# Layer-norm transposes by DMA, quotients before the layer norm, and a higher target for zero matmuls, in a fused attention and feed-forward kernel on one core

## The chip, the cores and the metric

The kernel runs on one core of one Trainium2 chip. The metric is the device time of one execution in microseconds (us). The record marks every run told of here as undisturbed ("fast"), so that all may be compared, and all kernels gave correct results. Names of engines in the profile: PE is the tensor engine's matmuls, PEld its weight loads, DVE the vector engine, ACT the scalar engine, POOL GpSimd, SP the engine whose queue issues nearly all DMAs here. A "q" behind an engine (SPq) is its sequencer, issuing.

## The reference, cut to what matters

```python
B, S, D, H = 1, 2048, 640, 32            # head width 20; F = 1728; bf16 inputs
def reference(x, wqkv, wo, w_gate, w_up, w_down):
    h  = x + attention(layernorm(x), wqkv) @ wo     # 32 heads, softmax over 2048 keys, no mask
    n  = layernorm(h)
    return h + ((n @ w_gate) * (n @ w_up)) @ w_down
```

Both layer norms feed matmuls that contract over D. Their outputs lie with tokens on the partitions, and the matmuls need D on the partitions, so each tile of 128 tokens x 640 must be transposed.

## The kernel before

A Python program plans the whole schedule with model clocks (`pe_t`, `dve_t`, `act_t`) and writes out each engine's instructions in one fixed order. Each engine works through its list in order. The foreground is attention: PE makes a block of scores, ACT exponentiates two or three blocks at a time (E), PE multiplies E with the values (acc). Some blocks are exponentiated on DVE instead. The background (`bg`) is a generator of PE work that fills gaps: first all projections to keys, queries and values ("keys stage" below, while the flag `ingest` is set), then, for each of five chunks of queries (512, 512, 384, 384, 256), the output projection, the second layer norm and the feed-forward.

A transpose on PE, with its copy out of PSUM on DVE:

```python
def transposed(ln_t, dst):
    ln, t = ln_t
    t += LN_SLACK if attn and left else 0.0
    while t + T_SEM > pe_t + 0.05:
        yield ("until", t + T_SEM)
    yield from m_wait()
    pt, rec = m_take(BF16, [P, KC, P])
    for c in range(KC):                                   # 5 transposes of 128x128
        nc.tensor.transpose(pt[:, c, :], ln[:, c * P:(c + 1) * P], ident[:])
    pe(0.3)
    m_done(rec, copy_out(dst, pt, 0.35))
    yield 0.3
```

The keys stage, one pass for each 512 tokens (`after(n, g)` runs g, then n pieces of the next pass's layer norm):

```python
fill_kq()                       # 72 DMAs of constant rows, all at the start
for ch in range(NCH):
    ...
    yield from after(2, proj_pad(0, ch, 1)); yield from after(2, proj_pad(1, ch, 1))   # keys
    ...
    yield from after(3, proj_v(t0 + 2, 0))                                             # values
    if more: yield from trans(t0 + TPC)
    yield from after(9, proj_v(t0 + 3, 0))
    if more:
        for t in range(1, TPC): yield from trans(t0 + TPC + t)
```

The end of a chunk (in `second_stage`), and the rule for zero matmuls in the main loop. Zero matmuls add nothing to acc; they are meant to keep PE busy so that its clock stays up. A debt of at least one bank (512 columns) first calls background work forward, and only when there is none makes zeros:

```python
done.add(("Wo", ci)); hurry = False
if ci == len(CHUNKS) - 2:
    load_last()                 # 8 DMAs of 320 KB: weights for the last chunk
load_w(0); load_w(1)            # 4 DMAs of 160 KB
... ln_stats; ln_finish; ln_recip
for tt in range(ntt):
    lns.append(ln_apply(L, tt, hs[tt], xr[:, tt, :]))
    if tt > 0: yield from transposed(lns[tt - 1], ln2T[...])
yield from transposed(lns[-1], ln2T[...])
# main loop
debt = min(max(0.0, debt + (HAM0 if ci == 0 else HAM) * (T1 - T0) / 2 * 2370 - cols), 3 * BK)
while True:
    if not blocked and bg and (pe_t < T1 + over and credit > 0 or debt >= BK):
        ...bg_step()
    elif debt >= BK and acc_t is not None and (pe_t < T1 + over or not warm_pe):
        cmm(acc_t, zeros[:, 0:P], zeros[:], False, False, skip_group_check=True)
    else: break
```

The quotients (attention sums divided by their denominators) go a roundabout way: acc is copied to accS (DVE), the denominators are sent by DMA into rs, inverted on DVE (rr), sent through DRAM to rb, and POOL multiplies accS by rb into on. There are two accS buffers.

The softmax here doesn't subtract the row's maximum and nothing guards it: scores larger than these inputs give would overflow.

Of the kernel before, what the change touches and what calls it, by code (L numbers as in the profile page):

```python
# [17 lines left out]
P = 128  # L18
# [5 lines left out]
G = H // HP  # L24
NT = S // P
KC = D // P
BK = 512
NCH = S // BK
TPC = BK // P
# [3 lines left out]
NG0 = 2  # L33
# [12 lines left out]
LN_SLACK = 2.0  # L46
D_V = 0.72
T_ON = (6.5, 16.0)
HAM0 = 0.5
EPS_B = 1.0013580322265625e-05  # L50

T_SW = 0.095
T_SEM = 0.2
# [6 lines left out]
HAM = 0.50  # L60
# [13 lines left out]
def kernel(  # L74
# [11 lines left out]
    nc = tc.nc  # L86
# [21 lines left out]
    pe_t = 0.0  # L108
    dve_t = 0.0
    act_t = 0.0  # L110
    mode = "F"
    cols = 0.0
    attn = False
    hurry = False
    ingest = True
# [103 lines left out]
            for ch in range(NCH):  # L219
                nc.gpsimd.dma_start(r_[:, ch, :], t_[:])  # L220

    def fill_kq():
        k_src = rowk[:].rearrange("r c q -> r (c q)")
        q_src = rowq[:].rearrange("r c q -> r (c q)")
        for g in range(NG0, G):
            for j in range(HP):
                r0, r1 = 32 * j + DH, 32 * j + 32
                nc.sync.dma_start(kT[g][r0:r1, :], k_src)
                nc.sync.dma_start(qT0[r0:r1, g, :], q_src[:, 0:q0w])
                nc.sync.dma_start(qT1[r0:r1, g, :], q_src[:, q0w:S])  # L230
# [45 lines left out]
    def ln_apply(L, i, s, ln):  # L276
        nc.vector.tensor_scalar(ln, s, L["mv"][:, i, 0:1], L["rstd"][:, i:i + 1],
                                ALU.subtract, ALU.mult)
        return ln, dve(0.36)
# [61 lines left out]
# [7 lines that stand above are left out]
        for c in range(KC):  # L348
            nc.tensor.transpose(pt[:, c, :], ln[:, c * P:(c + 1) * P], ident[:])  # L349
        pe(0.3)  # L350
        m_done(rec, copy_out(dst, pt, 0.35))
        yield 0.3


    def mm_qk(ps, lhs, ch):
        sl = slice(ch * BK, (ch + 1) * BK)
# [70 lines left out]
    done = set()  # L427
# [3 lines left out]
    def lnT_dst(t):  # L431
        return lnT[:, :, t * P:(t + 1) * P]
# [8 lines left out]
    dve_t = 4.0  # L441
    act_t = 8.0
    L = ln_new(TPC)
# [13 lines left out]
    lns = [ln_apply(L, t, xt[0][:, t, :], xt[0][:, t, :]) for t in range(TPC)]  # L457
# [8 lines left out]

    def first_stage():
        nonlocal ingest
        fill_kq()

        lns = []
        ahead = deque()

        def ln_ahead(ch):
            L = ln_new(TPC)
            x = [xt[ch][:, t, :] for t in range(TPC)]
            lns.clear()
            for t in range(TPC):
                ahead.append(lambda t=t: ln_stats(L, t, x[t]))
            ahead.append(lambda: ln_finish(L))  # L480
            ahead.append(lambda: None)
            ahead.append(lambda: ln_recip(L))
            for t in range(TPC):
                ahead.append(lambda t=t: lns.append(ln_apply(L, t, x[t], x[t])))

        def after(n, gen):
            yield from gen
            for _ in range(min(n, len(ahead))):
                ahead.popleft()()

        def trans(t):
            while len(lns) <= t % TPC:
                ahead.popleft()()
            return transposed(lns[t % TPC], lnT_dst(t))

        first_dense = NG0 * HP * DH // P
        f0 = first_dense
        for ch in range(NCH):
            t0 = ch * TPC
            more = ch + 1 < NCH  # L500
            if more:
                ln_ahead(ch + 1)
            if ch == 0:
                yield from after(1, proj_pad(1, 0, 1))
                yield from after(0, proj_v(0, 0))
                yield from after(1, proj_pad(1, 0, 0))
                yield from after(2, proj_v(1, 0))
            else:
                yield from after(2, proj_pad(0, ch, 1))
                yield from after(2, proj_pad(1, ch, 1))  # L510
                if not more:
                    yield from proj_dense(f0, [0], 0)
                yield from after(2, proj_v(t0, 0))
                if not more:
                    yield from proj_dense(f0, [0, 1], 1)
                yield from after(2, proj_v(t0 + 1, 0))
            yield from after(3, proj_v(t0 + 2, 0))
            if more:
                yield from trans(t0 + TPC)
            yield from after(9, proj_v(t0 + 3, 0))  # L520
            if more:
                for t in range(1, TPC):
                    yield from trans(t0 + TPC + t)
        ingest = False
        yield from proj_dense(f0, [2, 3], 1)
        for ft in range(f0 + 1, KC):
            yield from proj_dense(ft, [0], 0)
            yield from proj_dense(ft, [0, 1], 1)
            if ft == KC - 2:
                for t in range(TPC):  # L530
                    yield from proj_v(t, 1)
            yield from proj_dense(ft, [2, 3], 1)
            if ft == KC - 2:
                load_wo()
                for t in range(TPC, NT):
                    yield from proj_v(t, 1)
        for g in range(NG0):
            for ch in range(1, NCH):
                yield from proj_pad(g, ch, 0)
        for ft in range(f0, KC):  # L540
            yield from proj_dense(ft, [1, 2], 0)
            yield from proj_dense(ft, [3], 0)
# [41 lines left out]
    def second_stage(ci, q0, qw, xr):  # L584
# [68 lines left out]
                ln_stats(L, tt - 1, hs[tt - 1])  # L653
        done.add(("Wo", ci))
        hurry = False
        if ci == len(CHUNKS) - 2:
            load_last()
        load_w(0)
# [7 lines left out]
        for tt in range(ntt):  # L666
            calm()
            lns.append(ln_apply(L, tt, hs[tt], xr[:, tt, :]))
            if tt > 0:
                yield from transposed(lns[tt - 1], ln2T[:, :, (tt - 1) * P:tt * P])  # L670
        yield from transposed(lns[-1], ln2T[:, :, qw - P:qw])
        if end:
            yield "rest"
        yield ("until", dve_t + T_SEM)
        for f in range(NF):
            M = min(P, FF - f * P)
            if f + 2 < NF:
# [196 lines left out]
    def emit_PV(s):  # L874
# [16 lines left out]
        if last:  # L891
# [11 lines left out]
                normalise(ci, q0, qw, g, sums.pop((ci, g)), t)  # L903
            acc_t = None

    sums = {}

    last_sum = []
# [105 lines left out]
    while n < len(units):  # L1014
        if n >= 6:
            values(units[n - 6][-1][0])
        n_slot = n
        cols = 0.0
        T0 = act_t
        emit_exp(n)  # L1020
        pe_t = max(pe_t, T0)
        T1 = act_t
        if n + 1 < len(units):
            T1 += len(units[n + 1]) * BANK_ACT + FIX_ACT
        if left:
            pe_t = max(pe_t, act_t + T_SEM)
            emit_S(len(units))
            if not ingest and ring[0]["t"] <= pe_t and dve_t < act_t + D_AHEAD and len(dq) < 2 and len(left) > 5 * HP:
                start_D()
        values()  # L1030
        for z in list(later):
            if z[0] <= max(dve_t, act_t) and all(t in done for t in z[2]):
                later.remove(z)
                z[1]()
        pump(act_t + 0.5)

        ci = steps[min(pv_next, len(steps) - 1)][0]
        if left:
            rest = sum(1 for b in left if steps[b[0]][0] == ci)
            rate = RUSH0 if hurry or ci == 0 else RUSH * max(bgw, 5.0) / max(rest / 2.8, 4)  # L1040
        credit = min(credit + rate, max(5 * rate, 2.0))
        for i in range(0, min(LOOK, len(left)), HP):
            if not all(t in done for t in tags_of(left[i][0])):
                credit = max(credit, 2.0)
        debt = min(max(0.0, debt + (HAM0 if ci == 0 else HAM) * (T1 - T0) / 2 * 2370 - cols), 3 * BK)
        blocked = False
        over = (OVER, OVER2)[n % 2]
        while True:
            tick()
            if not blocked and bg and (pe_t < T1 + over and credit > 0 or debt >= BK):  # L1050
                c0 = cols
                c = bg_step()
                if isinstance(c, tuple):
                    blocked = c[1] > max(T1 + over, pe_t + 0.1)
                    pe_t = pe_t if blocked else max(pe_t, c[1])
                else:
                    credit -= c
                    bgw -= c
                    debt = max(0.0, debt - cols + c0)
                pump(act_t + 0.5)  # L1060
            elif debt >= BK and acc_t is not None and (pe_t < T1 + over or not warm_pe):

                cmm(acc_t, zeros[:, 0:P], zeros[:], False, False, skip_group_check=True)
                pe(0.216, "C")
                debt -= BK
            else:
                break
        pump(act_t + 0.9)
        n += 1
# [48 lines left out]
```

## Time and profile before

1008.31 us, the median of 3 runs (1008.09 to 1011.38). The profiled run took 1005.8 us, of which the profile covers a span of 1004.1.

| | before |
|---|---|
| ACT busy | 861 us, of it 849 in 745 exponentials |
| ACT idle from the 1st to the 52nd exponential (keys stage, 22 to 123 us) | 43 us |
| mean PE clock 21 to 123 us | 0.80 |
| after the last exponential | 57 us |

The first two parts of the page of the kernel before: busy time of each engine, then the span in 40 slices with busy tenths, and PEclk, the clock granted to PE in tenths.

```profile
PE 867.8 (86%) x14133; PEld 368.4 (37%) x14134; DVE 751.3 (75%) x1290; ACT 861.3 (86%) x776; POOL 226.1 (23%) x263
...
ACT  3466599799989999999999999999979999989701
...
PEclk8778889999999999999989989999989999999989
```

ACT is at 9 tenths over most of the span. In the first five slices, the keys stage, it is not. The table by stretch gives that in numbers (columns: stretch, its length, busy us of PE, PEld, DVE, ACT, POOL with instruction counts, clock, DMA share, GB/s).

```profile
25.00:50.00 25.00, 19.07 (x219) 7.47 (x211) 13.48 (x35) 10.90 (x11) 1.05 (x1) 0.73 0.27 76
50.00:75.00 25.00, 19.42 (x215) 7.32 (x211) 11.61 (x30) 15.16 (x13) 1.00 (x1) 0.73 0.02 6
75.00:100.00 25.00, 19.46 (x239) 8.07 (x239) 11.91 (x31) 16.97 (x15) 1.01 (x1) 0.86 0.01 1
100.00:125.00 25.00, 17.74 (x231) 6.47 (x223) 7.63 (x13) 13.74 (x13) 1.11 (x1) 0.85 0.06 13
375.00:400.00 25.00, 22.72 (x285) 7.65 (x284) 22.22 (x35) 25.00 (x23) 6.18 (x7) 1.00 0.35 85
```

In the first four stretches ACT works 10.9 to 17.0 us of 25 at a clock of 0.73 to 0.86; later it works 25.0 of 25 at a clock of 1.0. The table of waits says what ACT waited for (us in total, times, longest), and shows a wait at chunk ends.

```profile
ACT E L807 <- PE acc L884: 40.7, 19, 4.4
...
PE acc L884 <- DVE accS L898: 5.9, 2, 3.2
...
DVE accS L898 <- POOL on_339 L947: 3.6, 2, 1.9
```

The timeline shows how the keys of the second 512 tokens come about (start, length, engine, line, operation, tiles, count, and in brackets the idle time before it and what ended it).

```profile
42.25 1.15 DVE L277 TENSOR_SCALAR xw<-xw,mv,rstd 128x640 bf16<-128x640 bf16 x3
...
42.94 1.25 PE L349 MATMUL mt<-ident,xw 128*128 128x128 bf16 x10
...
45.72 2.75 PE L148 MATMUL mt<-lnT,Wp 128*32 128x512 bf16 x24 [0.58 <-DVE lnT L328]
...
49.82 1.45 ACT L807 ACTIVATE E<-sp 128x1536 bf16<-128x1536 f32 x1 [4.36 <-PE acc L884]
```

The last step of the layer norm (L277), the transposes of its tiles on PE (L349), and the key projection (L148), which waited for the last copy out of PSUM (lnT, L328), stand in a row; ACT resumes at 49.82 after 4.36 us. And this is the end of the third chunk:

```profile
737.56 0.85 POOL L266 TENSOR_TENSOR den<-ve,half 128x3 bf16<-128x3 bf16 x1 [7.93 <-DVE ve L263]
738.37 0.99 POOL L947 TENSOR_TENSOR on_339<-accS,rb 128x384 bf16<-128x384 f32 x1
...
739.40 0.56 DVE L898 COPY accS<-acc 128x384 f32<-128x384 f32 x1 [1.93 <-POOL on_339 L947]
...
740.01 0.80 PE L884 MATMUL acc<-E,Vx 128*32 128x384 bf16 x9 [3.18 <-DVE accS L898]
...
743.20 1.02 ACT L807 ACTIVATE E<-sp 128x1024 bf16<-128x1024 f32 x1 [4.57 <-PE sp L784]
```

The copy to accS at 739.40 waits for a buffer, which the quotient on_339 frees, and POOL runs that only after the layer norm's den. PE waits 3.18 us for the copy, and ACT 4.57 us for the scores behind it.

### The profile page before, as it was taken

The page shows a single profiled execution, that of the slowest core. Times are in us where ns is not written, and L with a number is a line of the kernel's source. Part 1 is how long each engine was busy: PE and PEld are TensorE (multiplying, and loading weights), DVE is VectorE, ACT ScalarE, POOL GpSimd, SP SyncE. Part 2 cuts the span into 40 slices and gives each one's busy share as a digit, 9 for nine tenths or more (in the row PEclk, how much of TensorE's full clock was granted, in tenths as well). Part 3 has the DMA queues.
Part 4 walks back from the last instruction along what each step waited for, and adds up shares of the span by engine and source line. Part 5 has one row for each costly group of instructions (what it writes and reads, how often), then busy time and mean ns, then how long its engine had stood idle before and what let it go on. Part 6 is the DMA issues. An engine that isn't in the chain of part 4 may idle for free.

```text
span 1004.1 us, 32961 instructions
## 1 busy us (share of the span) xinstructions
PE 867.8 (86%) x14133; PEld 368.4 (37%) x14134; DVE 751.3 (75%) x1290; ACT 861.3 (86%) x776; POOL 226.1 (23%) x263
## 2 busy tenths in 40 slices
PE   7777798789977989998988899989978999879988
PEld 3223222322222323223434333334433444434566
DVE  4544367678869798988788888888888887888542
ACT  3466599799989999999999999999979999989701
POOL 4000021222213132222232222322222222232100
PEclk8778889999999999999989989999989999999989
DMA  6200011301111113330010122301123311343304
GB/s 224 75 5 1 13 42 39 75 14 33 35 40 47 40 39 84 79 88 13 33 46 11 36 56 58 73 14 44 46 43 69 64 31 52 82 103 79 86 28 82
DMA packets 121916, 53.26 MB, mean 53 GB/s; under 512 B 98026, under 2 KB 117066, under 8 KB 121770
## 3 DMA queue, kind: packets, MB, share of 16 engines
q1 hardware_dynamic: 120794, 49.75, 20.8%
q8 instruction: 110, 1.80, 0.8%
q10 hardware_dynamic: 720, 1.31, 0.3%
q14 instruction: 36, 0.29, 0.1%
q0 software_dynamic: 256, 0.10, 0.0%
HBM read 43.47 MB, written 2.98 MB: 46 GB/s over the span
## 4 chain that ended last, share of the span: by engine, by line
ACT 40%; issue 23%; PE 21%; DVE 7%; SPq 4%; DMA 3%; POOL 1%; DVEq 0%; POOLq 0%; ACTq 0%
ACT E L807 40%; PE mt L148 10%; PE sp L784 5%; SPq L406 3%; PE acc L884 3%; PE acc L148 1%; DVE v L840 1%; PE mt L349 1%; DVE v L842 1%; DVE fx L834 1%; DVE ed L845 1%; POOL uc L837 1%; DMA rs<-accS 1%; DMA rd<-rr 1%; DVE Vx L328 1%
## 5 line engine op out<-in xcount | busy, mean ns | idle before, releaser
L807 ACT ACTIVATE E<-sp 128x1536 bf16<-128x1536 f32 x745 | 849.2, 1352 | 81.0 <-PE acc L884 40.7
L837 POOL TENSOR_SCALAR uc<-fx 128x512 f32<-128x512 uint16 x185 | 160.9, 870 | 587.0 <-DVE fx L834 561.1
L884 PE MATMUL acc<-E,Vx 128*32 128x256 bf16 (+3 forms) x2787 | 165.5, 321 | 7.9 <-DVE accS L898 5.9
L840 DVE SCALAR_TENSOR_TENSOR v<-fx 128x512 f32<-128x512 uint16 x185 | 156.0, 846 | 1.2
L834 DVE TENSOR_SCALAR fx<-mt 128x512 int32<-128x512 f32 x185 | 126.4, 684 | 32.9 <-PE mt L784 31.3
L842 DVE SCALAR_TENSOR_TENSOR v<-v,uc 128x512 f32<-128x512 f32 x185 | 129.5, 701 | 14.9 <-POOL uc L837 12.1
L845 DVE SCALAR_TENSOR_TENSOR ed<-fx,v 128x512 uint16<-128x512 int32 x185 | 133.7, 724 | 1.3
L884 PEld LDWEIGHTS <-Vx 128*32 128x32 bf16 x3072 | 57.9, 97 | 79.8 <-issue 72.3
L148 PE MATMUL mt<-ln2T,wg 128*32 128x512 bf16 (+1 forms) x1080 | 76.3, 360 | 1.0 <-DMA wg<-in_B_w_gate_dram 0.9
L148 PE MATMUL mt<-ln2T,wu 128*32 128x512 bf16 (+1 forms) x1080 | 73.7, 356 | 0.9 <-DVE gs L328 0.7
L884 PE MATMUL acc<-ed,Vx 128*32 128x256 bf16 (+3 forms) x285 | 69.2, 315 | 0.3 <-DVE ed L845 0.3
L148 PE MATMUL acc<-zeros 128*32 128x512 bf16 x676 | 62.3, 426 | 0.0
L328 DVE COPY gs<-mt 128x512 f32<-128x512 f32 (+3 forms) x54 | 33.6, 623 | 15.4 <-PE mt L148 15.3
L784 PE MATMUL sp<-qT_161,kT_152 32*128 32x256 bf16 (+3 forms) x284 | 29.2, 305 | 10.7 <-ACT E L807 10.4
L148 PEld LDWEIGHTS <-wu 128*32 128x32 bf16 x1190 | 27.2, 95 | 29.1 <-issue 17.9
L784 PE MATMUL sp<-qT_161,kT_155 32*128 32x256 bf16 (+3 forms) x287 | 29.6, 313 | 9.2 <-ACT E L807 8.7
L148 PEld LDWEIGHTS <-wg 128*32 128x32 bf16 x1190 | 27.4, 96 | 27.7 <-issue 17.6
L784 PEld LDWEIGHTS <-kT_153 32*128 32x128 bf16 x384 | 16.9, 92 | 53.4 <-issue 52.9
L784 PE MATMUL sp<-qT_161,kT_154 32*128 32x256 bf16 (+3 forms) x294 | 28.7, 292 | 8.8 <-ACT E L807 8.1
L784 PE MATMUL sp<-qT_161,kT_156 32*128 32x256 bf16 (+3 forms) x294 | 29.0, 292 | 8.0 <-ACT E L807 7.4
L324 ACT COPY gs<-mt 128x256 f32<-128x256 f32 (+3 forms) x16 | 6.2, 385 | 34.4 <-PE mt L148 34.4
L784 PE MATMUL sp<-qT_161,kT_158 32*128 32x256 bf16 (+3 forms) x291 | 28.3, 293 | 7.7 <-ACT E L807 6.8
(210 smaller groups left out, 1245.9 us busy)
## 6 DMA issues: line engine op xcount, KB each, us to landing
wg<-in_B_w_gate_dram SPq DMA_DIRECT2D x57, 160.0 KB
wu<-in_B_w_up_dram SPq DMA_DIRECT2D x57, 160.0 KB
rb<-rd SPq DMA_DIRECT2D x16, 256.0 KB
rb<-rd SPq DMA_DIRECT2D x16, 192.0 KB
out_dram<-xr SPq DMA_DIRECT2D x14, 160.0 KB
Wd<-in_B_w_down_dram SPq DMA_DIRECT2D x13, 160.0 KB
xr<-in_A_x_dram SPq DMA_DIRECT2D x2, 640.0 KB
qT_161<-in_B_w_gate_dram SPq DMA_DIRECT2D x4, 320.0 KB
```

The source lines that it names most:

```text
L148: nc.tensor.matmul(out[j:j + 32], lhsT=lhsT[:, j:j + 32], rhs=rhs, start=start, stop=stop, **kw)
L328: nc.vector.tensor_copy(dst, src)
L349: nc.tensor.transpose(pt[:, c, :], ln[:, c * P:(c + 1) * P], ident[:])
L406: nc.sync.dma_start(dst, tmp[lo - ft * P:hi - ft * P, 0:n])
L784: nc.tensor.matmul(out[:, c:c + n], lhsT=kT[g][32 * j:32 * j + 32, kt * P:(kt + 1) * P], rhs=q_of(g, q0 + qo, n)[32 * j:32 * j + 32, :], s ...
L807: nc.scalar.activation(E[:, 0:len(u), :], sp[:, 0:len(u), :], ACT.Exp, scale=LN2_ / UNIT, bias=-BIAS * LN2_ / UNIT)
L834: nc.vector.tensor_scalar_mul(fx[:], d["sp"], 512.0)
L837: nc.gpsimd.tensor_scalar(d["uc"][:], u, EXP_C, 0.0, ALU.mult, ALU.add)
L840: nc.vector.scalar_tensor_tensor(d["v"][:], d["u"], EXP_A, d["u"], ALU.add, ALU.mult)
L842: nc.vector.scalar_tensor_tensor(d["v"][:], d["v"][:], EXP_B, d["uc"][:], ALU.add, ALU.mult)
L845: nc.vector.scalar_tensor_tensor(e[:], d["fx"][:], 1.0 / 512.0, d["v"][:], ALU.mult, ALU.add)
L884: nc.tensor.matmul(acc_t[32 * j:32 * j + 32, qo:qo + n], lhsT=Vx[:, kt, h * VS:h * VS + 32], rhs=E_of[s, j][0][:, c:c + n], start=kt == k0 ...
```

## The change

Its intent: transposes leave PE and DVE and become DMA transposes on the SP queue (all but the first tiles and the last chunk's); the layer norm of the keys stage runs earlier and the filling of constant rows is split, so that the transposes don't stand behind 72 DMAs; quotients that are due are issued before the chunk's layer norm; and the target for zeros is 0.8 of PE's columns, but only in the keys stage.

```diff
-HAM0 = 0.5
+HAM0 = 0.8
+T_TR = 4.5
...
+    def transposed_dma(ln_t, dst):
+        nc.sync.dma_start_transpose(out=dst, in_=ln_t[0])
+        return ln_t[1] + T_TR
...                                                       # first_stage
-        fill_kq()
             for t in range(TPC):
-                ahead.append(lambda t=t: lns.append(ln_apply(L, t, x[t], x[t])))
+                def last(t=t):
+                    t_ln[ch] = transposed_dma(ln_apply(L, t, x[t], x[t]), lnT_dst(ch * TPC + t))
+                ahead.append(last)
         for ch in range(NCH):
+            while ahead:
+                ahead.popleft()()
+            while t_ln.get(ch, 0.0) > pe_t:
+                yield ("until", t_ln[ch])
+            fill_kq(range(min(NG0 + 2 * ch, G), min(NG0 + 2 * ch + 2, G)))
...                                                       # counts for after() of ch 0: 1,0,1,2 -> 2,1,2,3
-            yield from after(3, proj_v(t0 + 2, 0))
-            if more:
-                yield from trans(t0 + TPC)
-            yield from after(9, proj_v(t0 + 3, 0))
-            if more:
-                for t in range(1, TPC):
-                    yield from trans(t0 + TPC + t)
+            yield from after(4, proj_v(t0 + 2, 0))
+            yield from after(11, proj_v(t0 + 3, 0))
...                                                       # second_stage
         hurry = False
+        run_later()                                       # quotients that are due
...
-            if tt > 0:
+            if not end:
+                t = transposed_dma(lns[tt], ln2T[:, :, tt * P:(tt + 1) * P])
+            elif tt > 0:
                 yield from transposed(lns[tt - 1], ln2T[:, :, (tt - 1) * P:tt * P])
...
+        while t > pe_t:
+            yield ("until", t)
...                                                       # main loop
-        debt = min(max(0.0, debt + (HAM0 if ci == 0 else HAM) * (T1 - T0) / 2 * 2370 - cols), 3 * BK)
+        debt = min(max(0.0, debt + (HAM0 if ingest else HAM) * (T1 - T0) / 2 * 2370 - cols), 3 * BK)
```

More of the change, by code (lines that the diff above doesn't have):

```diff
@@ L220, in const_rows, with fill_kq @@
                 nc.gpsimd.dma_start(r_[:, ch, :], t_[:])
-    def fill_kq():
+    def fill_kq(gs):
         k_src = rowk[:].rearrange("r c q -> r (c q)")
         q_src = rowq[:].rearrange("r c q -> r (c q)")
-        for g in range(NG0, G):
+        for g in gs:
             for j in range(HP):
@@ L468, in first_stage @@
         nonlocal ingest
-        fill_kq()
-        lns = []
+        t_ln = {}
         ahead = deque()
@@ L476, in ln_ahead @@
             x = [xt[ch][:, t, :] for t in range(TPC)]
-            lns.clear()
             for t in range(TPC):
@@ L489, in after @@
                 ahead.popleft()()
-        def trans(t):
-            while len(lns) <= t % TPC:
-                ahead.popleft()()
-            return transposed(lns[t % TPC], lnT_dst(t))
         first_dense = NG0 * HP * DH // P
@@ L503, in first_stage @@
             if ch == 0:
-                yield from after(1, proj_pad(1, 0, 1))
-                yield from after(0, proj_v(0, 0))
-                yield from after(1, proj_pad(1, 0, 0))
-                yield from after(2, proj_v(1, 0))
+                yield from after(2, proj_pad(1, 0, 1))
+                yield from after(1, proj_v(0, 0))
+                yield from after(2, proj_pad(1, 0, 0))
+                yield from after(3, proj_v(1, 0))
             else:
@@ L668, in second_stage @@
             lns.append(ln_apply(L, tt, hs[tt], xr[:, tt, :]))
-            if tt > 0:
+            if not end:
+                t = transposed_dma(lns[tt], ln2T[:, :, tt * P:(tt + 1) * P])
+            elif tt > 0:
                 yield from transposed(lns[tt - 1], ln2T[:, :, (tt - 1) * P:tt * P])
-        yield from transposed(lns[-1], ln2T[:, :, qw - P:qw])
         if end:
+            yield from transposed(lns[-1], ln2T[:, :, qw - P:qw])
             yield "rest"
-        yield ("until", dve_t + T_SEM)
+            t = dve_t + T_SEM
+        while t > pe_t:
+            yield ("until", t)
         for f in range(NF):
@@ L904, in emit_PV, with run_later @@
             acc_t = None
+    def run_later():
+        for z in list(later):
+            if z[0] <= max(dve_t, act_t) and all(t in done for t in z[2]):
+                later.remove(z)
+                z[1]()
     sums = {}
@@ L1030 @@
         values()
-        for z in list(later):
-            if z[0] <= max(dve_t, act_t) and all(t in done for t in z[2]):
-                later.remove(z)
-                z[1]()
+        run_later()
         pump(act_t + 0.5)
```

## The prediction

> **What bounds it now.** Mostly ScalarE's exponentials: the page gives ACT 861 of 1004 us busy, and the table of 25 us windows shows ACT at 25.0 of 25 in most windows from 325 to 725 us. Its idle time lies in three places. (a) While keys are made (22 to 125 us) ACT is busy only 11 to 17 of each 25 us, about 43 us idle; the granted clock is 0.73 to 0.86 there, 1.0 later. The waits are 39 us for value products (E <- acc) and 10 us for scores. The chain of waits in 22 to 130 us holds 51 us of projections, scores and value products, 5.7 us of PE transposes, 1.9 us of their copies. (b) At ends of chunks: 4.6 us at 743, 3.9 us at 885. The timeline shows the copy of the sums (accS) waiting for the quotient on_339, which POOL runs only after the layer norm's den. (c) The tail after 945 us, which stays.
>
> **What the change does.**
> - Keys stage: 12 tiles lose 5 transposes (0.6 us of PE per tile) and a 0.49 us DVE copy. Each becomes a DMA transpose on the SP queue, planned at 4.5 us after the layer norm, which is issued earlier. Keys then wait for one landing, not for transposes and copies in series (chunk 1: layer norm ends 43.4, key projection starts 45.7, ACT resumes 49.8). With the layer norm 4 to 5 us sooner and the flight partly hidden behind value projections, I expect 3 to 5 us per chunk, 11 us for three.
> - Zeros: the target 0.5 becomes 0.8 in this stage; it also calls background work earlier. A 512-column matmul is 0.38 us warm, 0.61 to 0.63 cold in this trace; the Trainium skill's "TensorE: Matmul & The Clock Gate" (Part 1: The HAM clock gate) says that the clock follows recent activity. I expect the clock to rise from 0.8 to about 0.92: 7 us off the 51 (51 x (1 - 0.8/0.92)), less some 4 us of added zeros: net 3 us.
> - Later chunks: 14 tiles lose 0.6 us of PE and 0.48 us of DVE. PE has slack there; DVE's 7 us let 2 or 3 more blocks be exponentiated on DVE (2.9 us each), worth 1 us.
> - Quotients first: at 739 and 882 the copy of the sums can start 1.7 us sooner, and the score behind two transposes about 1 us sooner: 4 us together.
>
> Sum: 19 us, shaded to 17 for late landings. ScalarE's work hardly changes; the gain is its idle time.
>
> **Risk.** No trace here has a DMA transpose. The skill's "VectorE: DVE Perf Modes" (The three transpose paths) gives 1309 ns for 128x128 by DMA; five in series would be an estimated 6.5 us, over the planned 4.5. PE works in order, so late landings would stop scores too, in 7 places.
>
> **Prediction:** 991 us, 8 in 10 between 977 and 1003. Faster by over 2%: 0.40; within 2%: 0.56; slower: 0.04.
>
> **What would show it.** Right: ACT idle in 22 to 125 us falls by 12 us or more; clock there over 0.9; the first score of group 2 (122 us) comes about 14 us sooner; the waits of accS for on_339 vanish; transposes land within 4.5 us. Wrong: PE waiting for lnT or ln2T from DMA over 2 us per chunk; zeros on the chain over 6 us; SP issue over 1 us per transpose, delaying the sums' DMAs, so that ACT idles more at chunk ends or between 125 and 325 us.

## The result

996.31 us, the median of 4 runs (994.53 to 997.16), against 1009.09 of the kernel before (4 runs). The ratio is 0.9868, with a 95% interval of 0.9844 to 0.9891. Ratios here are the mean time of one kernel's runs over that of the other's runs of the same rounds, so they are not quite the ratio of the medians. The page of the changed kernel, the same lines:

```profile
PE 862.5 (87%) x14051; PEld 358.0 (36%) x14052; DVE 749.7 (75%) x1273; ACT 861.0 (87%) x775; POOL 232.4 (23%) x265
...
ACT  4486779999898999999999899999979999869701
...
PEclk8798789999998899999989999999979998979999
```

And its stretches while keys are made, where the stage now ends at 109 us and not at 123:

```profile
25.00:50.00 25.00, 18.33 (x208) 6.19 (x204) 13.11 (x35) 11.91 (x11) 1.05 (x1) 0.72 0.34 65
50.00:75.00 25.00, 18.99 (x283) 7.46 (x279) 14.40 (x41) 22.04 (x20) 2.01 (x2) 0.97 0.34 76
75.00:100.00 25.00, 19.27 (x254) 6.36 (x246) 7.83 (x14) 16.72 (x15) 0.00 (x0) 0.90 0.14 30
```

ACT's busy time is the same to 0.3 us; what fell is its idle time. The second stretch shows it best: ACT 22.0 us where it was 15.2, at a clock of 0.97 where it was 0.73. Over the whole run its waits for acc fell from 40.7 to 24.4 us, while those for scores (sp) rose from 32.7 to 41.1 us, and PE has new ones, for a transposed tile (table of waits of the changed kernel):

```profile
ACT E L813 <- PE acc L890: 24.4, 13, 3.2
...
PE mt L149 <- DMA ln2T<-xr: 9.4, 2, 6.9
```

What the trace has of the tile lnT in the changed kernel lists its DMA transposes by the tile that they read (time to issue one, min/median/max in ns, then first and last start in us):

```profile
L357 SPq DMA_TRANSPOSE lnT<-xw x4: 1201/1227/1337, 32.8 to 40.9; - x4
...
L357 SPq DMA_TRANSPOSE lnT<-x_97 x4: 1200/1227/1742, 72.6 to 78.4; - x4
```

And the same of the tile ln2T, in the chunks:

```profile
L357 SPq DMA_TRANSPOSE ln2T<-xr x14: 1215/1246/1725, 337.3 to 877.7; - x14
```

The SP queue needs about 1.2 us to issue one. Three in a row start at 1.3 us distance; where PE waited for the last of them, it started 2.8 us after that one's issue began.

**Where the time went.** All kernels run 744 to 746 exponentials in nearly the same sequence, so the n-th exponential is a clock on which two traces can be laid side by side. How much sooner it started in the changed kernel's profiled run (us, worked out from the two traces):

| exponential | 1st | 31st | 51st (first of group 2) | 183rd | 201st | 251st | 661st | 701st | end |
|---|---|---|---|---|---|---|---|---|---|
| sooner by | 1.6 | 10.6 | 13.9 | 21.1 | 22.2 | 14.2 | 14.6 | 5.1 | 8.9 |

So in this trace the change gained 14 us in the keys stage, as predicted, and 7 to 8 us more in the stretch after it, which I had not predicted; then it gave back 8 us around the first chunk's end and 9.5 us around the fourth's, and won 4 us after the 701st exponential. The second loss is easy to see in the timeline of the changed kernel (start, length, engine, line, operation, tiles, count, idle time before it and what ended it):

```profile
869.23 1.84 DVE L278 TENSOR_SCALAR xr<-h,mv,rstd 128x640 bf16<-128x640 f32 x3
...
871.20 1.00 SPq L606 DMA_DIRECT2D wu<-in_B_w_up_dram  x1
...
872.30 2.64 SPq L943 DMA_DIRECT2D rs<-accS  x4
...
875.04 3.92 SPq L357 DMA_TRANSPOSE ln2T<-xr  x3
...
880.47 0.83 PE L149 MATMUL mt<-ln2T,wg 128*32 128x384 bf16 x8 [6.85 <-DMA ln2T<-xr]
...
881.95 1.45 ACT L813 ACTIVATE E<-sp 128x1536 bf16<-128x1536 f32 x1 [7.27 <-PE sp L790]
```

The layer norm of all three tiles is done at 871.07. The three transposes start to be issued at 875.04, because loads of weights and the sums' DMAs stand ahead of them in the SP queue. From 863 us on the loads take 1.0 to 1.6 us each to issue, the four DMAs of the sums 2.64 us together. From the end of the layer norm to the tile's use 9.4 us pass, where the plan had 4.5. PE has the feed-forward's first matmul next in its list and stops for 6.85 us, scores behind it stop too, and ACT idles 7.27 us.

Such a lead is not measured to the last us, since each kernel has one trace. How far two traces differ can be seen from kernels whose program is the same up to there. In the kernel before, chunks_only, quot_only and wo_late (told of below) the first exponential came at 18.6 to 21.6 us and the 51st 101.6 to 105.0 us later. In the changed kernel, chunks_pe, keys_zeros, late_load and spread_load it came at 18.7 to 22.0 us and the 51st 89.3 to 92.4 us later. So the shorter keys stage is clear of this noise, but a difference of some 3 us between two kernels is not. late_load and spread_load have the changed kernel's program up to 860 us (the order of DMAs included). Their leads were 20.0 and 17.4 us at the 201st exponential and 14.6 and 14.5 at the 251st: what is given back there is anything from 3 to 8 us.

### The profile page after: what moved, and what is told of

Its sections match the earlier page's. It is cut to its first block, busy times and chain, and to the rows that moved or that the text cites. A ratio compares the mean times of both kernels' runs of the same rounds, so it can differ in the third digit from the quotient of the medians.

```text
span 995.2 us, 32806 instructions
## 1 busy us (share of the span) xinstructions
PE 862.5 (87%) x14051; PEld 358.0 (36%) x14052; DVE 749.7 (75%) x1273; ACT 861.0 (87%) x775; POOL 232.4 (23%) x265
## 4 chain that ended last, share of the span: by engine, by line
ACT 41%; PE 25%; issue 20%; DVE 7%; DMA 4%; SPq 3%; POOL 1%; POOLq 0%; DVEq 0%; ACTq 0%
ACT E L813 41%; PE mt L149 12%; PE sp L790 7%; PE acc L890 4%; SPq L412 3%; PE acc L149 1%; DVE st L254 1%; DVE ed L851 1%; DVE v L848 1%; DVE fx L840 1%; DMA rs<-accS 1%; DVE v L846 1%; DMA qT_161<-tmp 1%; DMA ln2T<-xr 1%; SPq L943 1%
## 5 line engine op out<-in xcount | busy, mean ns | idle before, releaser
L813 ACT ACTIVATE E<-sp 128x1536 bf16<-128x1536 f32 (+1 forms) x745 | 849.2, 1361 | 75.4 <-PE sp L790 41.1
L890 PE MATMUL acc<-E,Vx 128*32 128x256 bf16 (+3 forms) x2784 | 168.0, 325 | 5.7 <-DVE accS L904 3.5
L848 DVE SCALAR_TENSOR_TENSOR v<-v,uc 128x512 f32<-128x512 f32 x187 | 136.9, 735 | 11.0 <-POOL uc L843 7.9
L149 PE MATMUL mt<-ln2T,wg 128*32 128x512 bf16 (+1 forms) x1080 | 78.5, 368 | 11.7 <-DMA ln2T<-xr 9.4
L149 PE MATMUL mt<-ln2T,wu 128*32 128x512 bf16 (+1 forms) x1080 | 76.1, 362 | 0.1
L890 PE MATMUL acc<-ed,Vx 128*32 128x512 bf16 (+3 forms) x288 | 69.8, 313 | 1.6 <-DVE ed L851 1.6
L149 PE MATMUL acc<-zeros 128*32 128x512 bf16 x724 | 66.5, 422 | 0.0
L790 PE MATMUL sp<-qT_161,kT_155 32*128 32x256 bf16 (+3 forms) x290 | 30.6, 321 | 7.3 <-ACT E L813 7.2
L325 ACT COPY gs<-mt 128x256 f32<-128x256 f32 (+2 forms) x15 | 5.7, 380 | 32.1 <-PE mt L149 32.1
```

What stands on the lines that cost most here:

```text
L149: nc.tensor.matmul(out[j:j + 32], lhsT=lhsT[:, j:j + 32], rhs=rhs, start=start, stop=stop, **kw)
L790: nc.tensor.matmul(out[:, c:c + n], lhsT=kT[g][32 * j:32 * j + 32, kt * P:(kt + 1) * P], rhs=q_of(g, q0 + qo, n)[32 * j:32 * j + 32, :], s ...
L813: nc.scalar.activation(E[:, 0:len(u), :], sp[:, 0:len(u), :], ACT.Exp, scale=LN2_ / UNIT, bias=-BIAS * LN2_ / UNIT)
L848: nc.vector.scalar_tensor_tensor(d["v"][:], d["v"][:], EXP_B, d["uc"][:], ALU.add, ALU.mult)
L890: nc.tensor.matmul(acc_t[32 * j:32 * j + 32, qo:qo + n], lhsT=Vx[:, kt, h * VS:h * VS + 32], rhs=E_of[s, j][0][:, c:c + n], start=kt == k0 ...
```

## The experiments

Twelve kernels ran. All outputs are right. In each call the kernel before ran again on the same chip; its medians in the calls were 1004.8 to 1006.8 us, with runs from 999 to 1012, so an interval of a ratio is about 0.5% wide to each side.

| kernel | made from | ratio | 95% | median us | keys stage, us | ACT idle 641st to 721st exp. |
|---|---|---|---|---|---|---|
| before | | 1 | | 1005 to 1009 | 101.6 | 4.0 |
| changed | | 0.9868 | 0.984 to 0.989 | 996.3 | 89.3 | 12.5 |
| keys_only | before | 0.9828 | 0.978 to 0.988 | 990.2 | 91.3 | 10.9 |
| zeros_only | before | 0.9823 | 0.978 to 0.987 | 989.3 | 91.9 | 6.2 |
| chunks_only | before | 1.0106 | 1.005 to 1.016 | 1018.4 | 102.2 | 15.0 |
| quot_only | before | 1.0023 | 0.997 to 1.008 | 1009.2 | 105.0 | 7.0 |
| order_pe | before | 0.9870 | 0.982 to 0.992 | 993.6 | 99.1 | 8.1 |
| zeros_skip | zeros_only | 0.9960 | 0.989 to 1.003 | 999.7 | 96.5 | 6.2 |
| wo_late | before | 0.9975 | 0.991 to 1.004 | 1002.5 | 103.1 | 3.9 |
| no_zeros | changed | 0.9838 | 0.979 to 0.989 | 990.4 | 91.9 | 8.8 |
| chunks_pe | changed | 0.9859 | 0.980 to 0.992 | 991.7 | 89.7 | 6.6 |
| late_load | changed | 0.9897 | 0.985 to 0.994 | 996.2 | 92.4 | 12.8 |
| spread_load | changed | 0.9918 | 0.987 to 0.997 | 996.0 | 90.4 | 8.6 |
| keys_zeros | changed | 0.9884 | 0.985 to 0.992 | 993.1 | 89.9 | 6.1 |

"Keys stage" is the time from the 1st to the 51st exponential in the profiled run; it and the last column are worked out from the traces.

### The four parts alone

**keys_only**: the kernel before with the keys stage of the changed one (DMA transposes, earlier layer norm, split filling). The diff is that part of the change; the zeros stay at 0.5.

```diff
+ first_stage() as in the changed kernel, with transposed_dma
- HAM0 = 0.8
+ HAM0 = 0.5      (no run_later() in second_stage, chunks' transposes on PE)
```

> The kernel before with DMA transposes (and the layer norm order that goes with them) in the keys stage only; zeros at 0.5, quotients late, chunks' transposes on PE. Theory A (the gain is the keys stage's lost PE transposes and copies; the DMA transposes of later chunks give part of it back): the 51st exponential comes 10 to 15 us sooner than in the kernel before, as in the changed one, and the time is at or below the changed kernel's, ratio 0.978 to 0.988. Rival B (the gain is the zeros' and the clock's): the 51st exponential comes less than 5 us sooner, ratio over 0.993.

Measured 0.9828; the 51st exponential came 13.2 us sooner. This part alone gains about as much as the whole change: the intervals overlap. Theory A holds for it.

**zeros_only**: the kernel before with the target 0.8 in the keys stage.

```diff
-HAM0 = 0.5
+HAM0 = 0.8
-        debt = ... (HAM0 if ci == 0 else HAM) ...
+        debt = ... (HAM0 if ingest else HAM) ...
```

> The kernel before with the zeros' target 0.8 during the keys stage only. Theory A: the keys stage has the background work anyhow and few zeros are added (the changed kernel has 28 there, the one before 32), ratio 0.996 to 1.002. Rival B (warmer clock is the gain): clock in the keys stage over 0.9 and ratio under 0.993.

Measured 0.9823, and the 51st exponential came 12.5 us sooner. Theory A fell here: I had expected nothing. The stage has 44 zero matmuls instead of 32 (three more groups of four), and the clock from 19 to 112 us is 0.90; on the stretches of the stage that the changed kernel leaves at 0.72 (25 to 50 us) it is above 0.9.

**chunks_only**: the kernel before with DMA transposes in the chunks' feed-forward stages alone.

```diff
+            if not end:
+                t = transposed_dma(lns[tt], ln2T[:, :, tt * P:(tt + 1) * P])
+        while t > pe_t:
+            yield ("until", t)
```

> The kernel before with DMA transposes in the feed-forward stages of the first four chunks only. Theory A: late landings stop PE at chunk ends, above all at the last one, where loads and sums stand ahead of the transposes in the SP queue: ratio 1.000 to 1.010, with a wait of PE on ln2T of over 3 us at the last chunk end. Rival C (PE and DVE time spared there is worth more than late landings cost): ratio 0.990 to 0.998.

Measured 1.0106: this part alone costs 1%. The line of its table of waits (us in total, times, longest):

```profile
PE mt L149 <- DMA ln2T<-xr: 16.0, 4, 11.0
```

The end of the fourth chunk in the timeline of chunks_only:

```profile
889.62 3.06 SPq L942 DMA_DIRECT2D rs<-accS  x4
892.78 3.92 SPq L358 DMA_TRANSPOSE ln2T<-xr  x3
894.19 0.20 DVE L947 RECIPROCAL rr<-rs 128x8 f32<-128x8 f32 x1 [7.13 <-DMA rs<-accS]
...
898.22 1.15 PE L149 MATMUL mt<-ln2T,wg 128*32 128x384 bf16 x12 [10.99 <-DMA ln2T<-xr]
...
900.02 1.45 ACT L818 ACTIVATE E<-sp 128x1536 bf16<-128x1536 f32 x1 [10.96 <-PE mt L795]
```

PE stops for 10.99 us and ACT for 10.96 us. The transposes stand in the queue behind the sums' DMAs (rs, 889.62), and DVE's reciprocal had waited 7.13 us for these. So this chunk end is held up by the SP queue as a whole, not by the transposes alone. (keys_only, which has no DMA transposes in the chunks, idles 10.9 us there too: its PE waits 5.2 us for an accS copy. So the last column of the table is not a measure of late transposes alone.)

**quot_only**: the kernel before with due quotients issued before the layer norm.

```diff
         hurry = False
+        run_later()
```

> The kernel before with the quotients issued ahead of the layer norm only. Theory A, as predicted: the waits of the sums' copy on the quotient at 739 and 882 us vanish, 2 to 4 us less: ratio 0.995 to 0.999. Rival D (the copy then waits for something else): 0.999 to 1.002.

Measured 1.0023, the same within the interval. The wait of the accS copy for POOL is gone, as predicted, but the time is not. The third chunk's end in its timeline:

```profile
746.39 0.17 DVE L263 TENSOR_SCALAR ve<-vb 128x3 bf16<-128x3 bf16 x1
746.47 0.55 DVE L899 COPY accS<-acc 128x384 f32<-128x384 f32 x1
...
747.07 0.62 PE L885 MATMUL acc<-E,Vx 128*32 128x384 bf16 x8 [5.04 <-DVE accS L899]
...
749.18 1.02 ACT L808 ACTIVATE E<-sp 128x1024 bf16<-128x1024 f32 x1 [4.90 <-PE mt L785]
```

The copy of accS now starts at 746.47, right after ve: DVE works in order, and in its list the layer norm's statistics come first. PE waited 5.04 us for it, where it had waited 3.18 in the kernel before, and ACT 4.90 where it had been 4.57. The wait moved from POOL to DVE's place in line.

### What makes the keys stage shorter

**order_pe**: keys_only, but with the transposes back on PE, issued at the start of each pass.

```diff
-                    t_ln[ch] = transposed_dma(ln_apply(L, t, x[t], x[t]), lnT_dst(ch * TPC + t))
+                    t_ln[ch, t] = ln_apply(L, t, x[t], x[t])
...
-            while t_ln.get(ch, 0.0) > pe_t:
-                yield ("until", t_ln[ch])
+            if ch:
+                for t in range(TPC):
+                    yield from transposed(t_ln[ch, t], lnT_dst(t0 + t))
```

> The kernel before with the earlier layer norm and the split filling of constant rows of the changed keys stage, but transposes on PE with their copies on DVE; zeros 0.5, quotients late. Theory T (the keys stage's gain comes from taking transposes and copies from PE and DVE): the 51st exponential within 5 us of the kernel before, ratio over 0.993. Rival O (it comes from the order, the layer norm ready sooner): 9 us or more sooner, ratio under 0.988.

The 51st exponential came only 3.7 us sooner, which is theory T; the stage lasts 99.1 us against 91.3 in keys_only. The 7.8 us between the two are not the transposes' leaving PE and DVE alone, though: order_pe's plan has no zeros at all in the keys stage, where keys_only has 36 and the kernel before 32, and its clock there is 0.77 against 0.85. In zeros_skip below, 44 zeros are worth 4.6 us of the stage; an estimate from that gives up to 4 us to the missing 36. So, by single traces, some 4 to 8 of the stage's 10 us are the transposes, and how much the new order would gain with its zeros kept was not tested. The ratio, too, is 0.987, which theory T did not allow. The rest was gained after the keys stage, mostly by less idle time of ACT between the 51st and 241st exponential (9.1 us, where it is 16.6 in the kernel before).

**zeros_skip**: zeros_only with the same plan, but its zero matmuls of the keys stage not issued. The other engines' instructions are the same.

```diff
-                cmm(acc_t, zeros[:, 0:P], zeros[:], False, False, skip_group_check=True)
+                if not ingest:
+                    cmm(acc_t, zeros[:, 0:P], zeros[:], False, False, skip_group_check=True)
```

> The kernel with zeros at 0.8 in the keys stage alone, whose schedule is planned as there but whose 44 zero matmuls in the keys stage are left out; everything else is in the same order. Theory K (those zeros pay through the clock): the clock in the keys stage falls from 0.93 to 0.82 or less and the 51st exponential comes 7 us or more later than with them; ratio over 0.990. Rival O (they pay through the order: a higher target also calls keys and values forward): the 51st exponential stays within 3 us of that kernel's, ratio 0.979 to 0.987.

The zeros in the keys stage of zeros_only (stretch, length, busy and count of the zeros on PE, PEld and DVE, clock, DMA share, GB/s):

```profile
19.00:112.00 93.00, 3.98 (x44) 1.10 (x44) 0.00 (x0) 0.90 0.11 30
```

And the same of zeros_skip, whose stage ends later:

```profile
19.00:117.00 98.00, 0.00 (x0) 0.00 (x0) 0.00 (x0) 0.79 0.10 28
```

Without 44 matmuls that take 4 us the clock falls from 0.90 to 0.79, and the stage takes 96.5 us instead of 91.9 (one trace each), although PE has less to do. The 51st exponential came 6.7 us later, just short of the 7 of theory K, 2.1 of them already in the first one. The whole kernel has 0.996 where zeros_only has 0.982. So the zeros do pay through the clock; but against the kernel before (101.6 us with 32 zeros), 5 us of the stage's gain stay without any zeros. They go with the other thing that a higher debt does: it calls background work forward. (Zeros left aside, the first difference between PE's lists in zeros_only and in the kernel before is a projection that comes ahead of a score, at 28 us.) And the number of zeros alone does not set the clock: with 32 of them the four kernels with the old keys stage have 0.77 to 0.81, no more than zeros_skip without any.

**no_zeros**: the changed kernel with HAM0 back at 0.5.

```diff
-HAM0 = 0.8
+HAM0 = 0.5
```

> The changed kernel with the zeros' target back at 0.5. Theory S (zeros and the keys stage's DMA transposes, each worth 1.7% alone, take away the same idle time of ScalarE, so that together they are worth no more than one): ratio 0.984 to 0.991, the changed kernel's. Rival (their gains add, and something else hides it): 0.996 or more.

Measured 0.9838. The zeros, worth 1.8% alone, add nothing to the DMA transposes. The counts say why: the changed kernel has 28 zeros in its keys stage and this one 36. With the transposes gone the higher target is met by calling projections forward, so that there are even fewer zeros (here, too, the first difference between PE's lists is a projection, at 30 us). The clock is 0.83 (20 to 109 us); over the five kernels with this keys stage it is 0.79 to 0.83, so that a rise is hardly shown.

### The chunk ends

**chunks_pe**: the changed kernel with the chunks' transposes back on PE.

```diff
-            if not end:
-                t = transposed_dma(lns[tt], ln2T[:, :, tt * P:(tt + 1) * P])
-            elif tt > 0:
+            if tt > 0:
                 yield from transposed(lns[tt - 1], ln2T[:, :, (tt - 1) * P:tt * P])
```

> The changed kernel with the chunks' transposes back on PE (DMA transposes in the keys stage, zeros 0.8 and early quotients stay). Theory A (DMA transposes at chunk ends give back about 1%): ratio 0.974 to 0.982 and no wait of PE for ln2T. Rival C (they cost nothing in company of the rest): 0.984 to 0.990, as the changed kernel.

Measured 0.9859, which is the rival's figure: not to be told from the changed kernel. ACT's idle time at the last chunk end fell from 12.5 to 6.6 us, as theory A has it, but the median of 991.7 us is only 4.6 below the changed kernel's. It was run at another time.

**late_load**: the changed kernel with load_last after the chunk's transposes.

```diff
-        if ci == len(CHUNKS) - 2:
-            load_last()
         load_w(0)
...
+        if ci == len(CHUNKS) - 2:
+            load_last()
         while t > pe_t:
```

> The changed kernel with the eight loads of the last chunk's weights (320 KB each) issued after the transposes of the chunk before, no longer ahead of them. Theory Q (the 6.9 us wait of PE for ln2T at the last chunk end is the SP queue's backlog, in which these loads stand first): the wait falls to under 3 us, ratio 0.977 to 0.984. Rival L (the landing of a transpose itself is slow, or the sums' transfers hold it): the wait stays over 5 us, ratio 0.985 to 0.990.

The end of the fourth chunk in the timeline of late_load:

```profile
870.69 3.92 SPq L357 DMA_TRANSPOSE ln2T<-xr  x3
...
876.12 0.83 PE L149 MATMUL mt<-ln2T,wg 128*32 128x384 bf16 x8 [2.75 <-DMA ln2T<-xr]
...
888.27 0.46 SPq L604 DMA_DIRECT2D wg<-in_B_w_gate_dram  x1
...
891.95 1.52 PE L149 MATMUL mt<-ln2T,wg 128*32 128x384 bf16 x20 [3.32 <-DMA wg<-in_B_w_gate_dram]
...
894.11 1.45 ACT L813 ACTIVATE E<-sp 128x1536 bf16<-128x1536 f32 x1 [3.67 <-PE sp L790]
```

The transposes now go out at 870.69, the layer norm having ended at 870.81, and PE's wait for ln2T is 2.75 us. So the larger part of the 6.85 us was the queue's backlog, as theory Q says. But the time stays: 0.9897. The big loads now stand ahead of the small DMAs that are needed next. They hold the queue until 882.75; then it stands another 3.7 us (1.1 in the changed kernel) at the sums' DMA rb, which waits for rd to land. wg goes out only at 888.27, PE waits 3.32 us for it and ACT 3.67. The backlog moved. (This is the rival's ratio by the mechanism of theory Q.)

**spread_load**: the changed kernel with two of these loads at each of four steps of the feed-forward loop. The other engines' programs are the same.

```diff
             if f + 2 < NF:
                 load_w(f + 2)
+            if ci == len(CHUNKS) - 2 and f in (3, 5, 7, 9):
+                load_last(f - 3)
```

> The changed kernel with the eight loads of the last chunk's weights spread over the feed-forward loop of the chunk before, two at each of four steps. Theory Q (the SP queue's backlog is what the last chunk end loses by): the wait for ln2T is under 3 us as with the late loads and the new stop of 3.7 us that those caused goes, ScalarE's idle time from the 641st to the 721st exponential falls from 12.5 to 8 us or less, ratio 0.981 to 0.986. Rival: another wait takes its place, idle time over 10 us, ratio 0.987 to 0.991.

The longest wait for ln2T is 2.8 us, the second stop is gone, and ACT's idle time there fell from 12.5 to 8.6 us, a little more than the 8 that I had set. At the 701st exponential this kernel was 4 us better placed against the kernel before than the changed one. But 3 us of idle time turned up after the 721st, the first exponential of its profiled run was 2 us later, and the ratio is 0.9918, above the rival's. That the backlog makes the transposes late is shown; a gain in time is not.

### The stretch after the keys stage

The kernel before loses 4.81 us at 200 us. In its timeline:

```profile
190.16 3.76 SPq L931 DMA_DIRECT2D rs<-accS  x4
...
196.56 0.25 DVE L936 RECIPROCAL rr<-rs 128x16 f32<-128x16 f32 x1 [6.25 <-DMA rs<-accS]
...
199.85 1.45 ACT L807 ACTIVATE E<-sp 128x1536 bf16<-128x1536 f32 x1 [4.81 <-PE sp L784]
```

DVE sits idle 6.25 us for rs, and everything behind it in its list with it. The sums' DMAs went out at 190.16, behind eight DMAs that load the output projection's weights. chunks_only and quot_only, with the same order up to there, stop at the same place (4.02 and 4.65 us); keys_only, zeros_only and the changed kernel don't, but each has a stop of 3.5 to 4.4 us near 136 us, which the kernel before has not.

**wo_late**: the kernel before with these loads moved later in the SP queue and spread. The other engines' programs are the same.

```diff
-                load_wo()
...
         for g in range(NG0):
             for ch in range(1, NCH):
                 yield from proj_pad(g, ch, 0)
+                if ch < 3:
+                    load_wo(2 * g + ch - 1)
```

> The kernel before with the loads of the output projection's weights spread and moved 30 to 60 us later in the SP queue; the other engines' programs are the same. Theory R (in the kernel before, the sums' DMAs stand behind these loads in the SP queue, the reciprocal waits 6.25 us for them, and ScalarE stops for 4.8 us at 200 us; the kernels that gain have another order there, so some 5 us of the changed kernel's gain are this): the stop goes, ScalarE's idle time from the 51st to the 182nd exponential falls from 12.8 to 9 us or less, ratio 0.993 to 0.998. Rival: the stop is not the loads', and stays; ratio 0.999 to 1.002.

The stop is gone, and rr's waits for rs fell from 7.6 to 1.7 us. ACT's idle time from the 51st to the 183rd exponential (the expectation is one off in its count) fell from 12.8 to 10.3 us, not to 9. ACT's lines in the timeline of wo_late show the stretch in which the stop had been:

```profile
185.38 36.26 ACT L809 ACTIVATE E<-sp 128x1536 bf16<-128x1536 f32 x32 [1.19 <-PE sp L786]
224.49 2.53 ACT L809 ACTIVATE E<-sp 128x1536 bf16<-128x1536 f32 x2 [2.85 <-PE sp L786]
```

ACT works through from 185.38 with 32 exponentials to past 221 us. But from 125 us to the long stretch of work that starts near 230 us, its stops add up to 8.4 us, where they are 10.9 in the kernel before: of the 4.81 us, 2.4 are left as a gain, because other stops grew (2.12 where 1.51 was, 2.85 where 2.42 was, and three of 0.5 to 1.3 us). By the 301st exponential nothing of the gain was left, and the ratio of 0.9975 does not differ from 1 beyond the interval. So theory R is half right: the loads caused this stop, but removing it alone doesn't give 5 us.

### A version to beat both

**keys_zeros**: the two parts that gain alone, together, and nothing else.

```diff
  the changed kernel
-        run_later()
+  chunks' transposes on PE (as in chunks_pe)
```

> The changed kernel without its two parts that gained nothing alone: DMA transposes and zeros at 0.8 in the keys stage, with the chunks' transposes on PE and the quotients after the layer norm. Theory S (the two parts take away the same idle time, so together they are worth about one): ratio 0.978 to 0.985, beating the kernel before and the changed one (0.987) and level with either part alone (0.983 and 0.982). Rival (the gains add where nothing hides them): 0.972 or less.

Measured 0.9884, six runs, outside both ranges. It beats the kernel before, but it is not better than either part alone, and not better than the changed kernel. (It differs from chunks_pe only in run_later, and the lists of DVE, ACT and SP came out the same in both; chunks_pe had 0.9859. A quarter of a per cent is thus no difference here.) The best medians are those of zeros_only (989.3 us, two lines changed) and keys_only (990.2), but their intervals overlap that of the changed kernel, so that I call them level with it, not faster.

## Why the prediction was right or wrong

The time was right: 991 predicted, 996 measured, inside the range, and "within 2%" was the likeliest class. Its steps, one by one:

- **Keys stage, 11 us by DMA transposes: right.** The first score of group 2 came 13.8 us sooner (122.25, then 108.44; predicted about 14), and ACT's idle time in the stage fell from 43.2 to 30.6 us (predicted 12 or more). keys_only shows that the new keys stage without a higher target does it (32.7 us of idle time). Of this, by the estimate under order_pe, some 4 to 8 us are the transposes' leaving PE and DVE; the rest is the new order and the zeros that go with it, which order_pe does not separate. No wait for lnT shows in the changed kernel.
- **Zeros, "the clock to rise from 0.8 to about 0.92 ... less some 4 us of added zeros": wrong as written.** The clock was 0.83, in other traces of the same keys stage down to 0.79, and there were fewer zeros, not more (28 for 32). The higher target was met by work that it called forward. That the clock matters was right, and shown by zeros_skip; that zeros and transposes gain the same idle time was missed, and so was that two changed lines alone would have done for the whole gain.
- **Later chunks, "worth 1 us": the count was right, the sign wrong.** DVE took 187 blocks instead of 185. But the DMA transposes' wait behind other DMAs cost more: 1.06% alone, and ACT's idle time at the fourth chunk's end rose from 4.0 to 12.5 us (6.6 in chunks_pe). In company of the rest no cost in time is shown: chunks_pe is level with the changed kernel. The risk was named, and so were the tests "PE waiting for lnT or ln2T from DMA over 2 us per chunk", which came out for two of four chunks (9.4 us in all), and "SP issue over 1 us per transpose" (1.2 us).
- **Quotients first, 4 us: wrong.** quot_only gave 1.002. I took the wait that the table named, POOL's, for the only one; DVE's own order stood right behind it.
- **Landing: right for the wrong reason.** Late landings did stop PE, but not because five blocks take 6.5 us: a transpose of five blocks was there 2.8 us after its issue began. The queue ahead of it was long.
- **Not in the sum at all:** some 8 us more gained between the 51st and 201st exponential, and 8 us given back around the first chunk's end (6.5 to 9.0 and 3 to 8 in the three traces of the same program). The first is in part the stop at 200 us, which a new order avoided without being meant to; wo_late puts that at 2.4 us, and the rest stays open. The second shows in zeros_only too (5 us between the 201st and 251st), without any DMA transpose, so it is not theirs; its cause stays open.

That the sum was right to 5 us is therefore partly luck: in the trace the terms outside the sum are 8 us won, 8 us and 9.5 us lost, and 4 us won at the end, and together they left a loss of some 5 us.

What stays open: why order_pe gains as much as the changed kernel with a keys stage only 2.5 us shorter than before, less than two traces of one program differ by; how the keys stage's gain divides between transposes and order; and why gains that single traces show at one place are so often lost by the end. The schedule is planned from model times, so that any change gives every later instruction a new place; several us are won or lost in this way, which no run here could hold still.

## What to carry to other kernels

Count what stands ahead of a new DMA in its issue queue, not only what the DMA takes: here three transposes of 1.2 us issue each waited about 4 us behind loads of which eight were not needed soon, and moving those eight made the next small load late. Before adding up gains, ask whether they take away the same idle time; run each part alone, since a two-line part may give the whole and another part may cost. And when a wait is taken away, look at the next thing in that engine's own order, which may hold the work to the same moment.

## What the Trainium skill lacked or had wrong

- "VectorE: DVE Perf Modes", The three transpose paths, gives 1309 ns for a 128x128 transpose by DMA and nothing for larger ones, and no page gives the time from issue to use of a 128x640 one. Here one DMA transpose of 128x640 bf16, SBUF to SBUF, took the SP queue 1.20 to 1.25 us to issue as a rule (up to 1.74), three followed each other at 1.3 us, and PE could start 2.8 us after the last one's issue began. The prediction's estimate of five times 1309 ns was far too long.
- "DMA: Bandwidth & Descriptors", Issuing engines are not separate DMA queues, says that the time a sequencer needs to initiate a DMA "is usually small relative to the DMA itself". Here it was not small and decided a chunk's end: of the 2.8 us from a transpose's issue to its use 1.2 are the issue, three take 3.9 us, four small DMAs of 1 KB each (rs) 2.6 us, and each 160 KB load 1.0 to 1.6 us where many stand in a row (0.4 to 0.5 us is the median). No page has these times for this chip under such a load; the page's counts of cycles for issuing, in its part on trn3 B0, are not for this transpose and not for a long queue.
- "TensorE: Matmul & The Clock Gate", Part 1: The HAM clock gate, agrees with these traces in that the clock follows recent activity: a zero matmul of 512 columns takes 0.38 us warm and up to 0.63 cold. What no page has is how little filler can be enough: in one order of work, 44 zero matmuls with 4 us of PE time in a stretch of 93 us made the difference between a mean clock of 0.90 and 0.79, and 4.6 us of the stage. In another order 32 gave no more than 0.77 to 0.81.
